# Scatters declared as writes to rows of their own, one wait ahead of the readers, and the routing's counts four slots later

## The chip, the core and the metric

The kernel runs on one core of a Trainium2 chip. The time is that of one execution on the device, in microseconds (us). The engines are PE (matrix multiply, with PEld for its weight loads), DVE (vector), ACT (scalar), POOL (GpSimd, which also issues the indirect DMAs) and SP (which issues the plain DMAs). Each engine takes its own instructions in the order in which they were written, and waits on semaphores for the others and for DMAs.

## The reference

Three stages follow one another, on 3072 tokens of width 384:

```python
# attention with a decaying state, over 4 batches, 8 heads, 768 steps, head width 48
for t in range(S):
    cur = einsum('bhd,bhe->bhde', u * k_t, v_t)
    y[t] = einsum('bhd,bhde->bhe', r_t, state + cur)
    state = w_t * state + einsum('bhd,bhe->bhde', k_t, v_t)
# mixture of 8 experts, each token to one of them
logits = x @ w_gate + modality_bias[modality_id]
e_idx, gate_w = argmax(logits), softmax(logits)[e_idx]
for e in range(8):
    mask = e_idx == e
    out[mask] = gate_w[mask] * (relu(x[mask] @ w1[e]) @ w2[e])
# three projections, their maximum, and a last matmul
h = maximum(maximum(x @ v1, x @ v2), x @ v3); h = maximum(h, ...)
return h @ v_out
```

## The kernel before

**Attention** works on 24 tiles of 128 tokens (`attention`, loop over `i`). In iteration `i` the DVE scans the decays of tile `i + 2` (L729), finishes the output `x` of tile `i - 1` (L814), and PE forms the scores of tile `i + 1` (L761) and the output of tile `i` (L789). POOL has four things per tile: it masks the scores `am` of tile `i + 1` (L765, twice), multiplies `nat` of tile `i + 2` (L692, L693), and scales `nat` of tile `i + 1` by its sums `sh` (L702). `output(i)` on PE needs the masked `am`; the next tile's `x` (L814) needs L702. So a POOL that is late holds up both PE and DVE.

**Routing** runs beside it in batches of tiles (`route_batch`, batches of 8, 8, 3, 2 and 3 tiles). A batch is a generator, and `slot()` calls in each iteration advance it by a few steps; a `SLOT` that it yields ends the slot. On DVE it finds each token's expert, on PE it counts the tokens of each expert ahead of this one (L264, L265, into `cum`), and from that DVE computes `places`: the row that each token has in a list ordered by expert. POOL then writes for each tile 128 pairs (token, weight) into those rows of the DRAM tensor `order` by one indirect DMA (`scatter`, L293). At most two tiles are scattered per iteration, one in the middle and one at the end (`do_scatters(1)`). `order` has been filled once with a value out of bounds by a plain DMA from `zt`.

**Readers of `order`.** In iteration 21 (`e - 3`), `first_ids(0)` issues what is left of the first 16 tiles' scatters and reads the first ids by indirect gathers into `oi_all` (L1094); `first_rows` then gathers the token rows `xin` (L1105). After the attention, `chain` scatters the last 8 tiles. Then `first_block` gathers the ids `oe` of the extra tile `X` (L1094, index `idxx` from L371), its rows `xin`, and transposes them on PE (`x_part`, L1113) between two halves of the second expert tile's matmuls.

**The experts' blocks.** `first_block` runs the 8 experts' two matmuls over 13 tiles of 256 tokens; `second_block` runs the three projections and the last matmul over 512 tokens at a time. Each 128 tokens of the result go to `ob` on ACT (L1205) and by an indirect DMA of POOL to their rows of `out` (L1206).

Every scatter to `order`, and every one to `out`, writes a tensor whose rows are only known when it runs, so by the tracking of accesses each waits until the one before has landed.

Of the kernel before, what the change touches and what calls it, by code (L numbers as in the profile page):

```python
# [33 lines left out]
W2_FIRST = range(8)  # L34
RATE = (2, 6, 4)
LEAD = 2
GAP = 1

V_MIX = [(1, 6), (0, 0), (0, 1), (1, 7), (0, 2), (0, 3), (1, 8), (0, 4), (0, 5), (1, 9)]
V_OPS = (0, 7, 6, 1, (2, 2, 1, 0), 7, 3)  # L40
# [6 lines left out]
def kernel(ctx: ExitStack, tc: tile.TileContext, rkw_t, v_t, vrk, u, modality, w_gate, bias, w1, w2, v1, v2,  # L47
                              v3, v_out, out):
    nc = tc.nc
    PE, DVE, ACT, POOL, SP = nc.tensor, nc.vector, nc.scalar, nc.gpsimd, nc.sync  # L50
    B, NC, _, D, _, HP, _ = rkw_t.shape
    H, S = 2 * HP, NC * 128
    NT, DM = out.shape
    E, _, F = w1.shape
    F2 = v1.shape[1]
    NTILE = NT // 128
# [11 lines left out]
    NG = -(-E * TW // 128)  # L68
# [22 lines left out]

    xs = dram.tile([NT, DM], F32, name="xs")
    x2t = dram.tile([NTILE // 2, 128, KD, TW], F32, name="x2t")
    order = dram.tile([E * NT, 2], I32, name="order")
    lgps = lgpool.tile([128, 512], F32, name="lgps")

# [19 lines left out]
    idg = ct([128, NTILE, 2], I32, "idg")  # L116
# [17 lines left out]
    places = ct([128, NTILE], I32, "places")  # L134
# [8 lines left out]
    def constants_rest(es):  # L143
        tmp = pool(es, "ctmp", 1)
        mi = tmp.tile([NTILE, 128, 2], I32, name="mi")

        def loads():
            SP.dma_start(out=b0, in_=bias.rearrange("m e -> (m e)")[None, :].to_broadcast([128, 2 * E])
                         .rearrange("p (m e) -> p m e", m=2))
            SP.dma_start(out=mi, in_=modality.bitcast(I32).rearrange("(t p a) -> t p a", t=NTILE, a=2))  # L150

        def rows():

            mf = tmp.tile([NTILE, 128], F32, name="mf")
            msk = tmp.tile([128, NTILE, E], I32, name="msk")
            DVE.tensor_copy(mf, mi[:, :, 0])
            zt = tmp.tile([128, 2 * E * NT // 128], I32, name="zt")
            POOL.memset(zt, OOB)
            SP.dma_start(out=order.rearrange("(p f) a -> p (f a)", p=128), in_=zt)
            yield  # L160
            ps = lgps[:, 288:288 + NTILE]
            PE.transpose(out=ps, in_=mf, identity=ident[0:NTILE, 0:NTILE])
            on = tmp.tile([128, 128], F32, name="on")
            POOL.memset(on, 1.0)
            yield
            DVE.tensor_copy(msk, ps.unsqueeze(2).to_broadcast([128, NTILE, E]))
            POOL.tensor_copy(ones_bf, on)
            yield
            DVE.tensor_copy(brow, b0[:, 0:1, :].to_broadcast([128, NTILE, E]))
            POOL.affine_select(out=sut_bf, in_=ones_bf, pattern=[[1, 128]], compare_op=ALU.is_gt, fill=0.0, base=0,  # L170
                               channel_multiplier=-1)
            yield
            DVE.copy_predicated(brow, msk, b0[:, 1:2, :].to_broadcast([128, NTILE, E]))
            iota(iota8, [[1, E]])
            iota(ebase, [[NT, E]])
            yield
            iota(iota24, [[TW, NTILE // 2]])
            iota(pidx, [[0, 1]], 0, 1)
            iota(pids, [[128, 2 * EARLY]], 0, 1)
            POOL.memset(zero8, 0.0)  # L180
            POOL.memset(idg, 0)
            yield
            POOL.iota(idg[:, :, 0], pattern=[[128, NTILE]], base=0, channel_multiplier=1)
            iota(iota256, [[1, TW]])
            yield
            iota(posm, [[128, NTILE]], 0, 1)
            iota(posl.rearrange("p (t a) -> p t a", a=2), [[TW, NTILE // 2], [0, 2]], TW - 1)
            yield
            POOL.memset(oi_all, OOB)
            POOL.memset(oe, OOB)  # L190
            for d in d0c.values():
                yield
                POOL.memset(d, 1.0)
                POOL.memset(d[:, :, 0:1], 0.0)
        return loads, rows


    carry = {"t": None}
# [38 lines left out]
    scatters = []  # L237

    def route_batch(batch, then=(), lead=0):

        t0, nb = batch
        for _ in range(lead):
            yield SLOT
        lg = cut("lg", nb, E)
        DVE.tensor_tensor(out=lg, in0=logits[:, t0:t0 + nb, :], in1=brow[:, t0:t0 + nb, :], op=ALU.add)
        yield
        oh = cut("oh", E, nb + 1, BF16, E * (NBMAX + 1))
        ohx = cut("ohx", E, nb + 1, BF16, E * (NBMAX + 1))
        if t0:
            DVE.tensor_copy(oh[:, :, 0], carry["t"])  # L250
        else:
            DVE.memset(oh[:, :, 0:1], 0.0)
        got = []
        yield from argmax_onehot(oh[:, :, 1:nb + 1].rearrange("p e c -> p c e"), lg, nb, "r", got)
        ex = cut("ex", nb, E)
        ACT.activation(out=ex, in_=got[0], func=ACTF.Exp)
        DVE.tensor_tensor_scan(out=ohx.rearrange("p e c -> p (e c)"), data0=d0c[nb].rearrange("p e c -> p (e c)"),
                               data1=oh.rearrange("p e c -> p (e c)"), initial=0.0, op0=ALU.mult, op1=ALU.add)
        carry["t"] = ohx[:, :, nb]
        for _ in range(lead and GAP):  # L260
            yield SLOT
        yield
        cum = lgps[:, 192:192 + E * nb].rearrange("p (e c) -> p e c", e=E)
        PE.matmul(cum, lhsT=sut_bf, rhs=oh[:, :, 1:nb + 1], start=True, stop=False)  # L264
        PE.matmul(cum, lhsT=ones_bf, rhs=ohx[:, :, 0:nb], start=False, stop=True)  # L265
        got = [gen() for gen in then]
        for gen in got:
            next(gen)
        for _ in range(lead and GAP):
            yield SLOT  # L270
        yield
        for gen in got:
            yield from gen
        sm = cut("sm", nb, 1)[:, :, 0]
        DVE.tensor_reduce(out=sm, in_=ex, axis=AX.X, op=ALU.add)
        yield
        DVE.tensor_scalar(out=sm, in0=sm, scalar1=1e-9, scalar2=None, op0=ALU.add)
        yield
        DVE.reciprocal(idg[:, t0:t0 + nb, 1].bitcast(F32), sm)
        yield  # L280
        pc = cut("pc", E, nb, F32, E * NBMAX)
        DVE.tensor_tensor(out=pc, in0=cum, in1=ebase.unsqueeze(2).to_broadcast([128, E, nb]), op=ALU.add)
        yield
        DVE.tensor_tensor(out=pc, in0=pc, in1=oh[:, :, 1:nb + 1], op=ALU.mult)
        yield
        pf = cut("pf", nb, 1)[:, :, 0]
        DVE.tensor_reduce(out=pf, in_=pc.rearrange("p e c -> p c e"), axis=AX.X, op=ALU.add)
        yield
        pi = places[:, t0:t0 + nb]
        DVE.tensor_copy(pi, pf)  # L290

        def scatter(c):
            POOL.indirect_dma_start(out=order[:, :], out_offset=bass.IndirectOffsetOnAxis(ap=pi[:, c:c + 1], axis=0),  # L293
                                    in_=idg[:, t0 + c, :], in_offset=None, bounds_check=E * NT - 1, oob_is_err=False)
        scatters.extend([lambda c=c: scatter(c) for c in range(nb)])

    def do_scatters(n=NTILE):
        for sc in scatters[:n]:
            sc()
        carry["scattered"] = carry.get("scattered", 0) + len(scatters[:n])  # L300
        del scatters[:n]
# [721 lines left out]
    class Experts:  # L1023
# [167 lines left out]
        def m2(self, ids):  # L1191
# [11 lines left out]
            def done(q):  # L1203
                ob = self.next_of("ob")
                ACT.activation(out=ob, in_=ps[q][:, 0:DM], func=ACTF.Copy, scale=ids[q][:, 1:2].bitcast(F32))  # L1205
                POOL.indirect_dma_start(out=out[:, :], out_offset=bass.IndirectOffsetOnAxis(ap=ids[q][:, 0:1], axis=0),  # L1206
                                        in_=ob, in_offset=None, bounds_check=NT - 1, oob_is_err=False)
            n = len(ids)

            early = range(1)  # L1210
# [50 lines left out]

    def first_ids(j):
        do_scatters(max(0, NG - carry["scattered"]))
        for q in (2 * j, 2 * j + 1):
            ex.gather_ids(oi_all[:, q, :], idxg[:, q:q + 1])

# [36 lines left out]
    def until(what):  # L1303
        for got in work:
            if got == what:
                return

    def first_block(vw):
# [6 lines left out]
        for s, cur in enumerate(seq):  # L1315
# [16 lines left out]
                    vw(V_OPS[2])  # L1332
            if s == EARLY - 1:
                until("X")
                for half in range(2):
                    ex.gather_ids(X["oi"][half], idxx[:, half:half + 1])
                rows_of(X)
                until("rows")
                ids_of(EARLY)
                rows_of(T[EARLY])  # L1340
                until("end")
                ids_of(EARLY + 1)
# [47 lines left out]
    def rest():  # L1390
# [3 lines left out]
        with tc.If(lastv > 0):  # L1394
            badv = nc.values_load(ctl[0:1, 62:63], min_val=0, max_val=1)
            with tc.If(badv > 0):
                with ExitStack() as es:
                    attention_general(es)
                with ExitStack() as es:
                    run(plan(es))  # L1400
            with ExitStack() as es:
# [109 lines left out]
```

## Time and profile before

| | |
|---|---|
| median of 3 runs | 824.42 us (823.46 to 825.88) |
| profiled execution | 823.74 us, span from first to last instruction 821.7 us |
| PE busy | 736.3 us, 90% of the span |
| DVE busy | 516.8 us, 63% |
| ACT busy | 313.8 us, 38% |
| POOL busy | 350.4 us, 43% |
| mean granted clock of PE | 0.93 of full speed |

The attention lies in the first 245 us or so, the first block reaches to about 550 us, the second block to 805 us. The shares are averages over these three: PE is nearly always busy in the two blocks, and in the attention DVE is.

### The profile page before, as it was taken

The numbers are of one execution on the slowest core, as the hardware profiler recorded it, in microseconds if no ns is written. First come the engines' busy times: TensorE is split into PE (matmuls) and PEld (weight loads), VectorE is DVE, ScalarE is ACT, GpSimd is POOL, SyncE is SP. The second block draws the span as 40 slices with busy tenths as digits, with TensorE's granted clock in tenths as the row PEclk, the third lists the DMA queues.
The fourth block names the chain that finished last, engine by engine and source line by source line (L and its number), as shares of the span: only waits on it lengthen the run. The fifth ranks groups of instructions, "written<-read, shape, count | busy, mean of one in ns | idle before, by whom it ended". The sixth has DMA issues, their size and how long they took to land. (4 is left out here: it accounts for less than half of the span.)

```text
span 821.7 us, 13030 instructions
## 1 busy us (share of the span) xinstructions
PE 736.3 (90%) x4737; PEld 663.8 (81%) x4746; DVE 516.8 (63%) x975; ACT 313.8 (38%) x705; POOL 350.4 (43%) x386
## 2 busy tenths in 40 slices
PE   6889897777859599999999999899999999999991
PEld 3778787667749598999999998788898988889891
DVE  5899996599748278777778887962414234142320
ACT  5556444234303145566566653331221222122110
POOL 7598665655572367565557543521020100102000
PEclk8699887879669899999999999999999999999997
DMA  8778687458311132211111723301020100101000
GB/s 233 185 217 253 181 192 195 109 162 228 90 58 23 45 113 61 79 59 59 60 59 58 244 77 116 115 11 68 1 77 1 59 20 0 39 1 39 0 12 32
DMA packets 32382, 74.57 MB, mean 91 GB/s; under 512 B 5973, under 2 KB 19061, under 8 KB 32308
## 3 DMA queue, kind: packets, MB, share of 16 engines
q1 hardware_dynamic: 27508, 64.15, 28.3%
q0 software_dynamic: 4800, 9.49, 3.6%
q8 instruction: 39, 0.64, 0.4%
q14 instruction: 35, 0.29, 0.1%
HBM read 87.96 MB, written 14.38 MB: 125 GB/s over the span
## 5 line engine op out<-in xcount | busy, mean ns | idle before, releaser
L1186 DVE TENSOR_TENSOR w2r<-mm,w2r 128x512 f32<-128x512 f32 x72 | 49.7, 691 | 140.9 <-PE mm L1126 140.8
L1124 PE MATMUL mm<-w1h,vh 128*128 128x512 f32 x324 | 126.1, 389 | 3.4 <-DVE w2r L1186 3.4
L1206 POOL DMA_INDIRECT out_dram<-w2r,oi_all x24 | 26.1, 1086 | 241.6 <-ACT w2r L1205 201.3
L1126 PE MATMUL mm<-w1h,vl 128*128 128x512 f32 x324 | 127.6, 394 | 0.0
L1125 PE MATMUL mm<-w1l,vh 128*128 128x512 f32 x324 | 127.0, 392 | 0.0
L1125 PE MATMUL mm<-hl,w2h 128*128 128x256 f32 x312 | 89.5, 287 | 3.2 <-DVE hl L1138 3.1
L1126 PE MATMUL mm<-xh,w1l 128*128 128x256 f32 x312 | 90.1, 289 | 1.4 <-DVE w1l L484 1.4
L1126 PE MATMUL mm<-hh,w2l 128*128 128x256 f32 x312 | 89.4, 286 | 0.9 <-DVE w2l L484 0.6
L1124 PE MATMUL mm<-hh,w2h 128*128 128x256 f32 x312 | 89.7, 288 | 0.0
L1124 PE MATMUL mm<-xh,w1h 128*128 128x256 f32 x312 | 88.5, 284 | 0.0
L1125 PE MATMUL mm<-xl,w1h 128*128 128x256 f32 x312 | 88.3, 283 | 0.2 <-issue 0.2
L789 PE MATMUL yb<-nat,am 128*128 128x56 f32 x384 | 57.8, 312 | 23.2 <-DVE lh L816 10.7
L789 PEld LDWEIGHTS yb<-nat,am 128*128 128x128 f32 x384 | 54.7, 226 | 25.8 <-POOL am L765 22.3
L1124 PEld LDWEIGHTS mm<-w1h,vh 128*128 128x128 f32 x324 | 60.8, 188 | 17.9 <-DVE w2r L1186 4.7
L484 DVE TENSOR_TENSOR w1l<-w1r,w1h 128x512 fp32r<-128x512 f32 x66 | 52.9, 855 | 35.2 <-ACT w1h L482 16.6
L1188 ACT CAST w2h<-w2r 128x512 fp32r<-128x512 f32 x36 | 22.3, 620 | 132.6 <-DVE w2r L1186 132.6
L1125 PEld LDWEIGHTS mm<-w1l,vh 128*128 128x128 f32 x324 | 60.8, 188 | 13.8
L1126 PEld LDWEIGHTS mm<-w1h,vl 128*128 128x128 f32 x324 | 60.9, 188 | 12.2
L484 POOL TENSOR_TENSOR w2l<-w2r,w2h 128x384 fp32r<-128x384 f32 x40 | 45.7, 1146 | 44.9 <-ACT w2h L482 43.9
L1125 PEld LDWEIGHTS mm<-hl,w2h 128*128 128x128 f32 x312 | 60.3, 193 | 4.8 <-DVE hl L1138 4.8
L1126 PEld LDWEIGHTS mm<-xh,w1l 128*128 128x128 f32 x312 | 59.7, 191 | 4.9 <-DVE w1l L484 4.9
L1126 PEld LDWEIGHTS mm<-hh,w2l 128*128 128x128 f32 x312 | 60.1, 193 | 1.9 <-DVE w2l L484 1.4
(242 smaller groups left out, 1758.3 us busy)
## 6 DMA issues: line engine op xcount, KB each, us to landing
w1r<-in_moe_w_dram SPq DMA_DIRECT2D x10, 1536.0 KB
w2r<-in_moe_w_dram SPq DMA_DIRECT2D x10, 1536.0 KB
nat<-in_vrk_dram SPq DMA_DIRECT2D x24, 608.0 KB
tq<-in_rkw_t_dram SPq DMA_DIRECT2D x46, 288.0 KB
stg<-in_moe_w_dram SPq DMA_DIRECT2D x18, 384.0 KB
vt<-in_v_t_dram SPq DMA_DIRECT2D x24, 192.0 KB
x2t<-raw SPq DMA_DIRECT2D x12, 384.0 KB
w1r<-x2t SPq DMA_DIRECT2D x12, 384.0 KB
```

The costliest lines, as they stand in the source:

```text
L484: eng.tensor_tensor(out=lo, in0=src, in1=hi.bitcast(F32), op=ALU.subtract)
L789: PE.matmul(yb[:, h * DV:(h + 1) * DV], lhsT=s["am"][:, 4 * (h % 2) + h // 2, :], rhs=s["v"][:, h, :], start=(h == 0), stop=(first and h = ...
L1124: PE.matmul(oc, lhsT=wh[:, kk, sl], rhs=xh[:, kk, :], start=first and kk == 0, stop=False)
L1125: PE.matmul(oc, lhsT=wh[:, kk, sl], rhs=xl[:, kk, :], start=False, stop=False)
L1126: PE.matmul(oc, lhsT=wl[:, kk, sl], rhs=xh[:, kk, :], start=False, stop=last and kk == nk - 1)
L1186: DVE.tensor_tensor(out=hv, in0=o, in1=hv, op=ALU.max)
L1188: ACT.copy(self.h2h[:, c, :], hv)
L1206: POOL.indirect_dma_start(out=out[:, :], out_offset=bass.IndirectOffsetOnAxis(ap=ids[q][:, 0:1], axis=0), in_=ob, in_offset=None, bounds_c ...
```

## The change

The scatters to `order` are put into a group whose members don't wait for each other, and so are the scatters to `out` where four are issued together (`apart`). Two instructions are new on POOL. `carry["filled"]` overwrites one column of `zt` ahead of the first scatter, so that it follows the fill's DMA, which reads `zt`. `settle` overwrites the `places` of the tiles scattered so far; each scatter reads its `places`, so this memset waits until all of them have landed, and the gathers of ids behind it on POOL come after. `GAP` becomes a pair: a batch's two matmuls that count (L264, L265) are written four slots behind the scan that they need, in place of one.

```diff
-GAP = 1
+GAP = (4, 1)
...
             SP.dma_start(out=order.rearrange("(p f) a -> p (f a)", p=128), in_=zt)
+            carry["filled"] = lambda: POOL.memset(zt[:, 0:1], 0)
...
-        for _ in range(lead and GAP):
+        for _ in range(lead and GAP[0]):
             yield SLOT
         yield
         cum = lgps[:, 192:192 + E * nb].rearrange("p (e c) -> p e c", e=E)
...
-            POOL.indirect_dma_start(out=order[:, :], out_offset=bass.IndirectOffsetOnAxis(ap=pi[:, c:c + 1], axis=0),
-                                    in_=idg[:, t0 + c, :], in_offset=None, bounds_check=E * NT - 1, oob_is_err=False)
+            apart("order", POOL.indirect_dma_start(
+                out=order[:, :], out_offset=bass.IndirectOffsetOnAxis(ap=pi[:, c:c + 1], axis=0),
+                in_=idg[:, t0 + c, :], in_offset=None, bounds_check=E * NT - 1, oob_is_err=False))
...
+    def apart(group, ins):
+        tc.declare_no_dep(ins.ins, group=group, reason="other rows")
+        tc.add_to_no_dep_group(group, ins.ins)
+    def settle(a, b):
+        POOL.memset(places[:, a:b], 0)
     def do_scatters(n=NTILE):
+        if scatters and "filled" in carry:
+            carry.pop("filled")()
         for sc in scatters[:n]:
             sc()
...
+                if n == 4:
+                    apart("out", ins)
...
     def first_ids(j):
         do_scatters(max(0, NG - carry["scattered"]))
+        if j == 0:
+            settle(0, NG)
...
                 until("X")
+                settle(NG, NTILE)
                 for half in range(2):
                     ex.gather_ids(X["oi"][half], idxx[:, half:half + 1])
```

The rows below are instructions of POOL in the order in which they stand, with the semaphores that each waits for. `DMASW0` to `DMASW7` are eight semaphores that POOL's own DMAs take in turn, and `Pool`, `DVE` and `Activation` are the engines' (the number behind them is the core's). First, two tiles of the attention around the first scatters, before:

```order
L293 DMA order_68<-idg_82,places_102 24576x2
L765 AFFINE_SELECT am_1309<-am_1309 128x512 [waits Activation_49] x2
L692 TENSOR_TENSOR nat_1239<-nat_1239,u_b_156 128x384 [waits DMAHW3_49]
L693 TENSOR_TENSOR nat_1239<-nat_1239 128x384 [waits Pool_49]
L293 DMA order_68<-idg_82,places_102 24576x2 [waits DMASW0_49]
L702 TENSOR_TENSOR nat_1142<-nat_1142,sh_1363 128x448 [waits DVE_49,Activation_49]
L293 DMA order_68<-idg_82,places_102 24576x2 [waits DMASW1_49]
L765 AFFINE_SELECT am_1398<-am_1398 128x512 [waits Activation_49] x2
```

The same place now:

```order
L781 AFFINE_SELECT am_1303<-am_1303 128x512 [waits Activation_49] x2
L708 TENSOR_TENSOR nat_1235<-nat_1235,u_b_156 128x384 [waits DMAHW3_49]
L709 TENSOR_TENSOR nat_1235<-nat_1235 128x384 [waits Pool_49]
L163 MEMSET zt_430 128x1
L297 DMA order_68<-idg_82,places_102 24576x2 [waits DVE_49]
L718 TENSOR_TENSOR nat_1142<-nat_1142,sh_1361 128x448 [waits DVE_49,Activation_49]
L297 DMA order_68<-idg_82,places_102 24576x2
L781 AFFINE_SELECT am_1396<-am_1396 128x512 [waits Activation_49] x2
```

The first scatter stands one slot (half a tile) later, the waits of one scatter for the last are gone, and the memset of `zt` is new.

Second, iteration 21 with `first_ids(0)`, before and now:

```order
L693 TENSOR_TENSOR nat_2148<-nat_2148 128x384 [waits Pool_49]
L293 DMA order_68<-idg_82,places_102 24576x2 [waits DMASW5_49]
L293 DMA order_68<-idg_82,places_102 24576x2 [waits DMASW6_49]
L1094 DMA oi_all_103<-order_68,idxg_95 128x2 [waits DMASW7_49]
L1094 DMA oi_all_103<-order_68,idxg_95 128x2
L702 TENSOR_TENSOR nat_2051<-nat_2051,sh_2297 128x448 [waits DVE_49,Activation_49]
```

```order
L709 TENSOR_TENSOR nat_2146<-nat_2146 128x384 [waits Pool_49]
L297 DMA order_68<-idg_82,places_102 24576x2 [waits DMASW5_49]
L297 DMA order_68<-idg_82,places_102 24576x2 [waits DMASW6_49]
L297 DMA order_68<-idg_82,places_102 24576x2 [waits DMASW7_49]
L309 MEMSET places_102 128x16 [waits DMASW4_49,DMASW5_49,DMASW3_49,DMASW6_49,DMASW2_49,DMASW7_49,DMASW1_49,DMASW0_49]
L1110 DMA oi_all_103<-order_68,idxg_95 128x2 x2
L718 TENSOR_TENSOR nat_2049<-nat_2049,sh_2299 128x448 [waits DVE_49,Activation_49]
```

Three scatters are left here instead of two. Each still names a semaphore, but with 16 scatters on eight semaphores in turn it is that of the scatter eight places ahead of it, not of the last one. The memset of `places` waits for all eight.

Third, the last 8 scatters and the gather of `oe` for the extra tile, before and now:

```order
L293 DMA order_68<-idg_82,places_102 24576x2 [waits DMASW3_49]
L293 DMA order_68<-idg_82,places_102 24576x2 [waits DMASW4_49,DVE_49]
L293 DMA order_68<-idg_82,places_102 24576x2 [waits DMASW6_49,DMASW5_49]
L293 DMA order_68<-idg_82,places_102 24576x2 [waits DMASW7_49,DMASW6_49]
L1094 DMA oe_104<-order_68,idxx_101 128x2 [waits DMASW7_49,DVE_49]
```

```order
L297 DMA order_68<-idg_82,places_102 24576x2
L297 DMA order_68<-idg_82,places_102 24576x2 [waits DVE_49]
L297 DMA order_68<-idg_82,places_102 24576x2 [waits DMASW6_49]
L297 DMA order_68<-idg_82,places_102 24576x2 [waits DMASW7_49]
L309 MEMSET places_102 128x8 [waits DMASW4_49,DMASW5_49,DMASW3_49,DMASW6_49,DMASW2_49,DMASW7_49,DMASW1_49,DMASW0_49]
L1110 DMA oe_104<-order_68,idxx_101 128x2 [waits DVE_49]
```

Here too the waits of one scatter for the one ahead are gone and one wait for all of them stands ahead of the gather.

## Rows read from the trace of the kernel before

**Rows 1.** Windows: busy us of each engine (instructions), granted clock, DMA share, GB/s.

```profile
core 0: us, PE busy (x) PEld busy (x) DVE busy (x) ACT busy (x) POOL busy (x), PEclk, DMA share, GB/s
47.65:88.86 41.21, 36.66 (x336) 33.10 (x336) 40.59 (x82) 24.25 (x72) 35.80 (x41) 1.00 0.85 235
88.86:107.63 18.77, 16.62 (x113) 15.57 (x112) 18.29 (x46) 8.10 (x25) 11.73 (x11) 0.70 0.73 194
113.43:165.69 52.26, 40.83 (x294) 37.36 (x294) 36.84 (x70) 21.34 (x63) 29.09 (x33) 0.83 0.70 166
165.69:204.67 38.98, 30.51 (x234) 27.00 (x235) 37.81 (x96) 15.48 (x47) 22.77 (x21) 0.85 0.71 185
204.67:245.17 40.50, 28.92 (x152) 23.81 (x153) 25.19 (x59) 7.88 (x20) 25.58 (x30) 0.65 0.26 76
278.50:288.77 10.27, 1.21 (x8) 1.20 (x7) 0.00 (x0) 0.85 (x2) 6.09 (x8) 0.61 0.06 16
287.57:292.00 4.43, 4.43 (x25) 4.43 (x26) 2.75 (x7) 1.43 (x4) 3.66 (x6) 0.61 0.02 1
```

**Rows 2.** The scatters' line: durations (ns), idle before them (us, times), landing.

```profile
L293 POOL DMA_INDIRECT order<-idg,places x24: 971/1008/1746, 109.7 to 276.7; - x24
...
  DMA order<-idg,places: 52.6, 16
...
DMA to landing us min/median/max: 3.6/8.6/9.0
```

**Rows 3.** Waits of DVE from 113.43 to 165.69: us, times, longest.

```profile
DVE x L814 <- POOL nat L702: 7.1, 3, 3.8
DVE sh L698 <- POOL nat L693: 5.6, 3, 2.1
```

**Rows 4.** Timeline of POOL, one tile of that stretch: start, us, instruction, idle before.

```profile
136.89 1.01 POOL L293 DMA_INDIRECT order<-idg,places  x1 [2.11 <-DMA order<-idg,places]
137.92 1.22 POOL L765 TENSOR_SCALAR_AFFINE_SELECT am<-am 128x512 f32<-128x512 f32 x2
139.11 0.99 POOL L692 TENSOR_TENSOR nat<-nat,u_b 128x384 f32<-128x384 f32 x1
...
145.53 1.01 POOL L293 DMA_INDIRECT order<-idg,places  x1 [4.36 <-DMA order<-idg,places]
146.57 0.94 POOL L702 TENSOR_TENSOR nat<-nat,sh 128x448 f32<-128x448 f32 x1
```

**Rows 5.** Timeline from the last scan (204.67) to the first block's first matmul.

```profile
207.40 1.07 ACT L764 COPY am<-mm 128x512 f32<-128x512 f32 x2 [0.23 <-PE mm L761]
...
222.28 1.01 POOL L293 DMA_INDIRECT order<-idg,places  x1 [0.43 <-DMA order<-idg,places]
...
226.48 0.97 POOL L293 DMA_INDIRECT order<-idg,places  x1 [3.20 <-DMA order<-idg,places]
230.41 1.04 POOL L1094 DMA_INDIRECT oi_all<-order,idxg  x1 [2.96 <-DMA order<-idg,places]
...
232.78 0.94 POOL L702 TENSOR_TENSOR nat<-nat,sh 128x448 f32<-128x448 f32 x1
...
235.79 1.19 POOL L1105 DMA_INDIRECT xin<-xs,oi_all  x1 [0.16 <-POOL xin L1101]
...
238.32 0.95 POOL L702 TENSOR_TENSOR nat<-nat,sh 128x448 f32<-128x448 f32 x1
...
240.25 0.56 DVE L814 TENSOR_TENSOR xe<-yb,nat 128x384 f32<-128x384 f32 x1 [0.95 <-PE yb L795]
...
245.17 0.38 PE L1124 MATMUL mm<-xh,w1h 128*128 128x256 f32 x1
```

**Rows 6.** Timeline around the extra tile.

```profile
257.78 0.16 DVE L371 SCALAR_TENSOR_TENSOR idxx<-pl_out,pl_gx 128x2 int32<-128x2 f32 x1
...
281.31 1.05 POOL L1094 DMA_INDIRECT oe<-order,idxx  x1 [3.63 <-DMA order<-idg,places]
...
287.57 1.54 PE L1113 MATMUL tp<-ident,xin 128*128 128x128 f32 x6 [9.06 <-DMA xin<-xs,oe]
```

**Rows 7.** Timeline at the end: the last result on ACT and its scatter on POOL.

```profile
804.54 0.58 ACT L1205 ACTIVATE w2r<-tp,oi_all 128x384 f32<-128x384 f32 x1 [2.54 <-PE tp L1201]
806.81 0.97 POOL L1206 DMA_INDIRECT out_dram<-w2r,oi_all  x1 [2.38 <-DMA out_dram<-w2r,oi_all]
```

More of the change, by code (lines that the diff above doesn't have):

```diff
@@ L268, in route_batch @@
             next(gen)
-        for _ in range(lead and GAP):
+        for _ in range(lead and GAP[1]):
             yield SLOT
@@ L1205, in done @@
                 ACT.activation(out=ob, in_=ps[q][:, 0:DM], func=ACTF.Copy, scale=ids[q][:, 1:2].bitcast(F32))
-                POOL.indirect_dma_start(out=out[:, :], out_offset=bass.IndirectOffsetOnAxis(ap=ids[q][:, 0:1], axis=0),
-                                        in_=ob, in_offset=None, bounds_check=NT - 1, oob_is_err=False)
+                ins = POOL.indirect_dma_start(out=out[:, :],
+                                              out_offset=bass.IndirectOffsetOnAxis(ap=ids[q][:, 0:1], axis=0),
+                                              in_=ob, in_offset=None, bounds_check=NT - 1, oob_is_err=False)
+                if n == 4:
+                    apart("out", ins)
             n = len(ids)
@@ L1398, in rest @@
                     attention_general(es)
+                settle(0, NTILE)
                 with ExitStack() as es:
```

## The prediction

> **What bounds the kernel now.** I read the windows by stage first, cut where a tile's first scan (L729) starts, then the scatters' line, then the waits of DVE and the timeline at the places where POOL stands still. In the attention before any scatter, six tiles take 41.21 us, 6.87 each, and DVE is busy for 40.59 of them: DVE is the bound there, with the DMA engines close behind at a share of 0.85 [rows 1]. When the first eight tiles are scattered, five tiles take 52.26 us, 10.5 each, and DVE is busy for only 36.84 [rows 1]. What happened is on POOL: in 16 places a scatter waited for the landing of the one before, 52.6 us in all, since a landing took 8.6 us at the median [rows 2]. In the tile shown the second scatter stands idle for 4.36 us and L702 comes only behind it [rows 4], and DVE's next tile needs L702: 7.1 us of DVE's idle time ended with L702 and 5.6 with L693, the other product of the same late POOL [rows 3]. So in this stretch the path runs over POOL's waits. It does so again from 204.67, where DVE is busy for 25.19 of 40.50 us [rows 1] and POOL waits 3.20 and 2.96 us between scatters and gathers before it comes to L702 [rows 5], and at the extra tile, where PE itself waits 9.06 us for rows whose ids were gathered behind the last scatter [rows 6]. In the two long blocks POOL's waits lie beside PE, but for the very last scatter [rows 7].
>
> **The change part by part.** Two scatters per tile remain as instructions of 1.01 us [rows 2]; what goes is the idle time ahead of them.
>
> *The scattered tiles, 113.43 to 165.69.* DVE was idle for 52.26 - 36.84 = 15.4 us, and 12.7 of these ended with POOL [rows 1, 3]. POOL's own work per tile, without waits, is 1.22 for the two L765, 0.99 for each of L692 and L693, 0.94 for L702 and 2.02 for two scatters, 6.2 us [rows 4], less than the 7.4 that DVE was busy per tile here. If DVE becomes the bound again, all 15.4 us go. Against that, the DMA engines were busy for 0.70 of 52.26, 36.6 us, and the same loads and scatters would have to fit in 36.8: two resources are nearly full at once. I take 7.85 us per tile, a gain of 13; the ends are 15.4 and the 5.3 of the first rival.
>
> *The counts four slots later.* PE no longer meets L264 ahead of the scan that it needs. But DVE is busy for 18.29 of 18.77 and 37.81 of 38.98 us around the first two batches [rows 1], so at most 1.65 us of idle time can go; I take 1. `places` and the number of the first expert come half a tile later, and one more scatter is left for iteration 21. If nothing covered the half tile it would cost 3.4 us once; the weights' loads stand an iteration behind, which covers it. Ends: a gain of 4, if what DVE does in small steps then meets POOL less often, and a loss of 3.4. The memset of `zt` and the two of `places` cost some 0.3 us each on POOL beside their waits, an estimate: the 0.16 us that an instruction starts behind its releaser [rows 5], and as much again for a column or a few of integers.
>
> *The end of the attention, from the last scan at 204.67.* The masked scores can start when ACT is done at 208.47, 3.8 us behind the scan [rows 5]. With POOL no longer a tile late, L765, L692 and L693 take it to 7.1. Three scatters, 1.3 us apart as issued, put the start of the last at 9.8. The new wait needs its landing: two scatters here stood 4.2 us apart, 222.28 and 226.48, with each waiting for the one before [rows 5], which gives 14.0, and 14.3 behind the memset. The two gathers take 2.4 as before (230.41 to 232.78), so L702 starts at 16.7. From it to the next L702 it took 5.5 (238.32), from there to `xe` 1.9, and from `xe` to the first matmul of the block 4.9 [rows 5]: 29.0 us in place of 40.5, a gain of 11.5. Ends: 13.5, if landing takes the 3.6 of the quickest and PE is at the higher clock level sooner, and 7, if it takes 8.6 [rows 2].
>
> *The extra tile.* Its ids need the last 8 scatters landed and `idxx`, which DVE has 12.6 us into the block (257.78) [rows 6]. The scatters, no longer 4 us apart, are then all but issued; with 1.3 for the last, 4.2 for landing and the 6.3 us from the gather of `oe` to PE's first transpose (281.31 to 287.57) the rows are there some 24 to 25 us into the block, and PE asks for them at 278.50, 33.3 into it. The whole wait of 9.06 goes. After it the granted clock averaged 0.61 over 4.43 us [rows 1], that is, partly at the lower level, which cost 4.43 x 0.39 = 1.7. Gain 10.8. Even a landing of 9.0 us leaves this slack; were there none, up to 9.06 would come back.
>
> *The scatters of the result.* Twenty-four of them lose waits, but PE doesn't wait for them. Only the last is on the path: ACT is done with it at 805.12 and it starts at 806.81 [rows 7]. It would start some 0.3 behind ACT; gain 1.4.
>
> The sum is 13 + 1 + 11.5 + 10.8 + 1.4 = 37.7 us. The profiled execution took 823.74 us, so 786.0; the median of the runs is 0.7 above it, so I say 786.5.
>
> **The rivals.** *POOL without waits gets in DVE's way.* DVE was busy for 6.77 us per tile without scatters and 7.37 with two [rows 1], so something of a scatter may already be paid on DVE. If each scatter stopped DVE for its whole 1.01 us, ten of them would turn 36.84 into 46.9 and leave 5.3 of the 15.4 us: 794. That it was 0.6 per tile and not 2.0 speaks against it; that POOL was idle for nearly half of this stretch (busy 29.09 of 52.26), so that the two met less often, speaks for it. The Trainium skill, "SBUF — State Buffer", section "Who interferes with whom", has a rule that would do this: GpSimd and VectorE share a pair of SBUF ports under an exclusive lock, and the second to come is blocked for the whole instruction. By that rule the rise of 0.6 us is what one would look for, though the trace does not show what caused it. Chance 0.16.
>
> *The new wait takes the place of the old.* The first memset of `places` waits for landings; at the median's 8.6 us in place of 4.2 the end of the attention gains 7 instead of 11.5: 791. For it: 8.6 is the median [rows 2]. Against it: the DMA share from 204.67 on is 0.26, against 0.70 where landings were slow [rows 1]. Chance 0.10.
>
> *Slower.* Scatters that nothing paces take the DMA engines from the attention's loads, and every tile waits for its data. To undo 37.7 us and add the 2.5 that a measurement of this kernel can tell (0.3%), each of 24 would have to cost the loads 40 / 24 = 1.7 us of all 16 engines. The share of 0.70 with two scatters per tile, below the 0.85 without [rows 1], speaks against a cost of that size. Then 827 or more. Chance 0.03.
>
> *No change.* The waits that were named were not what landed last, and others (loads, PE) end at the same times. The 12.7 us that DVE waited for POOL and the 9.06 of PE speak against it. Chance 0.02. *More than the sum:* DVE's small steps get shorter in the routing stretches too, and the ends above come together at 45 us: 779 or less. Chance 0.09.
>
> **How the numbers follow.** What I forecast, 780 to 793, has 0.60, and that is its own range; its price is the sum. With the two rivals above it and most of the one below, 777 to 802 leaves out less than 2 in 10; 802 is 5.3 for the scattered tiles, a loss of 2 for the counts, 7 for the end of the attention, 10.8 and 1.4. Faster by over 0.3%: 0.60 + 0.16 + 0.10 + 0.09 = 0.95; within it 0.02; slower 0.03.
>
> **What would show it.** After the change, the idle time of L297 (the scatters' new line) that ends with a DMA should be near zero; the five scattered tiles should take 39 us and DVE be busy for 95% of them; from the last scan to the first matmul of the block should be about 29 us, with one wait of some 3 us at the memset of `places`; the wait of PE at the extra tile should be gone and the clock stay at its higher level there; the last scatter should start within 0.3 us of ACT. I am wrong if DVE's busy time in the scattered tiles grows by as much as its idle time falls, if PE or DVE wait for loads there, or if the memset of `places` waits for 8 us.

## The result, and the profile after

The changed kernel took 790.72 us at the median (789.26 to 794.78, 4 runs), the kernel before, beside it, 825.15. The ratio is 0.9585, 95% interval 0.9535 to 0.9635. Run again beside some of its variants (e7, below), it was 0.9648 (0.9623 to 0.9673), and that is the figure for comparisons with them. The profiled execution took 794.78 us, the longest of the four, with a span of 792.5 in place of 821.7.

First the stages, cut where a tile's first scan (now L745) starts: six tiles before any scatter, three with the first routing ([rows 1] has two of them), the five scattered ones, four more, and from the last scan to the first block's first matmul.

```profile
45.83:87.05 41.22, 36.76 (x338) 33.10 (x336) 40.60 (x83) 24.14 (x72) 35.81 (x41) 1.00 0.85 232
87.05:111.97 24.92, 21.04 (x168) 19.30 (x167) 24.37 (x58) 10.99 (x34) 16.04 (x16) 0.86 0.66 181
111.97:152.57 40.60, 37.02 (x290) 34.13 (x289) 38.60 (x71) 21.01 (x62) 36.55 (x35) 0.83 0.90 198
152.57:191.56 38.99, 29.59 (x227) 26.87 (x226) 37.84 (x93) 16.00 (x48) 27.91 (x25) 0.84 0.79 201
191.56:225.37 33.81, 24.82 (x161) 20.21 (x160) 19.98 (x62) 7.85 (x20) 21.85 (x26) 0.73 0.38 85
```

The five tiles went from 52.26 to 40.60 us, and DVE is busy for 95% of them. But its busy time rose too, from 36.84 to 38.60, and POOL's to 36.55, 7.3 per tile. The end of the attention went from 40.50 to 33.81, less than I had said.

The scatters' line shows that the waits between scatters are gone, all 52.6 us of [rows 2]. What is left, 10.3 us in 2 places, is waited for by the two memsets of `places` (L309):

```profile
L297 POOL DMA_INDIRECT order<-idg,places x24: 972/1010/1864, 113.1 to 236.8; - x24
...
  issue: 4.4, 20
  DVE pl_cgs L374: 1.8, 1
...
  POOL places L309: 10.3, 2
...
DMA to landing us min/median/max: 3.3/5.6/11.5
```

Most of these 10.3 us fall where it hurts, as the timeline of the attention's end shows (compare [rows 5]):

```profile
194.67 0.96 SPq L1278 DMA_DIRECT2D w2r<-in_moe_w_dram  x2
...
202.23 0.98 POOL L297 DMA_INDIRECT order<-idg,places  x1 [0.30 <-issue]
...
202.71 0.37 SPq L1278 DMA_DIRECT2D w2r<-in_moe_w_dram  x1
...
210.02 0.11 POOL L309 MEMSET places<- 128x16 int32 x1 [6.82 <-DMA order<-idg,places]
210.80 1.05 POOL L1110 DMA_INDIRECT oi_all<-order,idxg  x1 [0.67 <-issue]
...
213.19 0.94 POOL L718 TENSOR_TENSOR nat<-nat,sh 128x448 f32<-128x448 f32 x1
...
214.17 0.56 DVE L830 TENSOR_TENSOR x<-yb,nat 128x384 f32<-128x384 f32 x1 [8.37 <-POOL nat L718]
...
225.37 0.38 PE L1140 MATMUL mm<-xh,w1h 128*128 128x256 f32 x1
```

The last of the first 16 scatters starts at 202.23 and the memset only at 210.02: 7.8 us. Behind it on POOL stand the gathers of ids and L718, and DVE waits 8.37 us for L718. The chain of work that ended last runs this way: the landing, the gathers, L718, DVE, PE. Three loads of w2 were issued close by.

At the extra tile, and at the last result ([rows 6, 7]):

```profile
241.51 0.10 POOL L309 MEMSET places<- 128x8 int32 x1 [3.51 <-DMA order<-idg,places]
...
258.57 0.82 PE L1129 MATMUL tp<-ident,xin 128*128 128x128 f32 x6
...
776.47 0.58 ACT L1221 ACTIVATE w2r<-tp,oi_all 128x384 f32<-128x384 f32 x1 [2.60 <-PE tp L1217]
777.33 0.97 POOL L1222 DMA_INDIRECT out_dram<-w2r,oi_all  x1 [2.21 <-ACT w2r L1221]
```

PE takes the extra tile's rows without a wait, where it had waited 9.06 us, and over the 4.43 us from there the granted clock was 1.00 (0.61 before). The last scatter starts 0.28 us behind the end of ACT (776.47 + 0.58), where it was 1.69.

The ledger of the spans, the change's first profile and a second one (e7, below) against the one of before; each stretch is a difference of two starts in the timelines. "The other routed tiles" are the three ahead of the five scattered ones and the four behind them:

| stretch | predicted gain | first | second |
|---|---|---|---|
| start to the scan of tile 11 | 0 | 1.8 | 0.0 |
| the five scattered tiles | 13 | 11.7 | 10.7 |
| the other routed tiles (counts) | 1 | -0.4 | -0.4 |
| last scan to the first matmul of the block | 11.5 | 6.7 | 6.9 |
| from there to the last result on ACT | 10.8 | 8.3 | 9.7 |
| the last result to the end | 1.4 | 1.1 | 1.3 |
| sum | 37.7 | 29.2 | 28.2 |

So 8.5 and 9.5 us of the sum are missing: nearly 5 at the end of the attention, 1.3 and 2.3 in the five tiles, 1.4 in the counts, and the rest in the blocks. By the medians the gain was 34.4 us in the first comparison, where the profiled execution was the slowest of the four, and 28.0 in the second.

### The profile page after: what moved, and what is told of

It reads as the page before. It is cut to its first block, busy times and chain, and to the rows that moved or that the text cites. A ratio compares the mean times of both kernels' runs of the same rounds, so it can differ in the third digit from the quotient of the medians.

```text
span 792.5 us, 13036 instructions
## 1 busy us (share of the span) xinstructions
PE 724.9 (91%) x4745; PEld 654.8 (83%) x4746; DVE 516.7 (65%) x975; ACT 313.5 (40%) x705; POOL 359.4 (45%) x389
## 4 chain that ended last, share of the span: by engine, by line
issue 37%; PE 23%; DVE 22%; DMA 7%; POOL 7%; ACT 2%; SPq 1%; POOLq 0%; ACTq 0%; DVEq 0%
PE mm L1142 7%; PE mm L1141 6%; PE mm L1140 6%; DMA tq<-in_rkw_t_dram 5%; POOL out_dram L1222 3%; DVE w1l L500 3%; DVE prod L745 2%; DVE prod L761 2%; DMA nat<-in_vrk_dram 1%; DVE rt L754 1%; DVE hl L1154 1%; DVE x L830 1%; DVE w2l L500 1%; DMA order<-idg,places 1%; DVE ya L528 1%
## 5 line engine op out<-in xcount | busy, mean ns | idle before, releaser
L1142 PE MATMUL mm<-w1h,vl 128*128 128x512 f32 x324 | 126.0, 389 | 0.0
L500 DVE TENSOR_TENSOR w1l<-w1r,w1h 128x512 fp32r<-128x512 f32 x66 | 52.1, 843 | 34.7 <-ACT w1h L498 34.6
L805 PE MATMUL yb<-nat,am 128*128 128x56 f32 x384 | 53.4, 299 | 16.4 <-DVE lh L832 13.9
L805 PEld LDWEIGHTS yb<-nat,am 128*128 128x128 f32 x384 | 51.0, 214 | 18.4 <-POOL am L781 9.0
L500 POOL TENSOR_TENSOR w2l<-w2r,w2h 128x384 fp32r<-128x384 f32 x40 | 45.7, 1146 | 45.0 <-ACT w2h L498 43.9
```

Of the source, the lines that this page charges most:

```text
L500: eng.tensor_tensor(out=lo, in0=src, in1=hi.bitcast(F32), op=ALU.subtract)
L805: PE.matmul(yb[:, h * DV:(h + 1) * DV], lhsT=s["am"][:, 4 * (h % 2) + h // 2, :], rhs=s["v"][:, h, :], start=(h == 0), stop=(first and h = ...
L1142: PE.matmul(oc, lhsT=wl[:, kk, sl], rhs=xh[:, kk, :], start=False, stop=last and kk == nk - 1)
```

## The experiments

All are variants of the changed kernel unless said otherwise; ratios are to the kernel before, run on the same chip. There were three chips: one for e1, e2, e3 and e6, one for e4, e5, e7 and e8, and one for e9. So e7 stands beside e4, e5 and e8 directly, and beside the others only by the ratios. The medians of before were 823.5 to 824.4 us, so 0.001 is 0.8 us.

**The change once more (e7).**

> The change itself, for the comparison with its variants on one chip, and for one question: in its profiled execution the last block's matmuls of 128x384 came every 176.4 ns, against 173.6 before, and the stretch from the block's first matmul to the last result was 2 to 3 us longer than in the variants with the same code there. Theory: that belongs to the one execution, and here the pitch is 173.6 or less and the span about 790 us. Rival: it belongs to the change, and shows again. Ratio in both cases 0.9585 within 0.004.

Ratio 0.9648 (0.9623 to 0.9673), above the bound that I gave (0.9625); the span was 793.6, not 790. The last matmuls came every 172.9 ns (the mean over 14 of them in the timeline). From the first result on ACT to the last it was 254.0 us here, 253.9 before, and 255.4 in the first profile of the change. Of all eleven profiles only that one and e4's have 255.4, the others 253.9 to 254.6, with the same matmuls there. So these 1.5 us belong to the execution.

**The last 8 scatters tied again (e1).**

```diff
-            apart("order", POOL.indirect_dma_start(
+            ins = POOL.indirect_dma_start(
...
+            if t0 < NG:
+                apart("order", ins)
```

> The changed kernel with the last 8 scatters of order back in order, each waiting for the landing of the one before, as in the kernel before; the first 16 and the scatters of the result stay free. Theory (my sum): the extra tile was worth 10.8 us, so this kernel takes about 790.7 + 10.8 = 801.5 us, a ratio of 0.971 to the kernel before, and PE waits some 9 us for the extra tile's rows again. Rival: the two traces show only 8.3 us less from the first matmul of the block to the last result, so the wait was worth less than I said: 799 us, 0.968. Second rival: the extra tile's rows would now come in time anyway, since the block's first ids come earlier; then there is no wait at the extra tile and the time stays at 791 us, 0.958.

Ratio 0.9761 (0.9734 to 0.9788), with the change at 0.9648 in such a comparison. PE waits again, now 10.80 us:

```profile
251.09 0.97 POOL L297 DMA_INDIRECT order<-idg,places  x1 [4.55 <-DMA order<-idg,places]
255.54 0.97 POOL L297 DMA_INDIRECT order<-idg,places  x1 [3.48 <-DMA order<-idg,places]
...
266.35 1.54 PE L1131 MATMUL tp<-ident,xin 128*128 128x128 f32 x6 [10.80 <-DMA xin<-xs,oe]
```

From the block's first matmul to the last result it takes 561.5 us, against 549.7 in e7 and 551.1 in the first profile: 10.4 to 11.8, as the sum had it (10.8). Both rivals are out. By the ratios the whole differs by 0.0113, or 9.3 us; in the profiles the end of the attention was 3 us shorter in e1 (30.55) than in e7 (33.57).

**No scatter in the five tiles (e6), and the same kernel timed (e8).** The two scatters of an iteration, one in the middle and one at its end, become two at each of these places, from iteration 17 on (the same edit at both):

```diff
-                if i < NTILE - 3:
-                    do_scatters(1)
+                if 17 <= i < NTILE - 3:
+                    do_scatters(2)
```

> The changed kernel with no scatter in the five tiles that had two each; they are issued two to a slot from iteration 17 on. Theory: the scatters on POOL lengthen DVE's instructions beside them (the scan L745 took 1.60 us there and 1.48 in the tiles without scatters; DVE was busy 7.7 us per tile), so without them the five tiles take 36 to 38 us instead of 40.6 and L745 falls back to 1.48 or less. Rival: what lengthens DVE there is POOL's other work (L709, L781), which keeps its place: L745 stays at 1.6 us and the five tiles at 40 us or more. Where the scatters come in pairs, later, the tiles get longer by what two cost; the whole is within 1% of the change.

The five tiles took 35.41 us in place of 40.60, 7.08 each, for 8 scatters less. The rows of DVE and POOL in these tiles, by line and shape (busy us, mean ns), of the change:

```profile
L745 DVE TENSOR_TENSOR_SCAN prod<-tq,d1f 128x512 f32<-128x512 f32 x6 | 9.6, 1596 | 0.0
L761 DVE TENSOR_TENSOR_SCAN prod<-tq,d1r 128x511 f32<-128x511 f32 x5 | 8.5, 1702 | 0.0
L730 DVE TENSOR_SCALAR tq<-tq 128x512 f32<-128x512 f32 x5 | 3.7, 743 | 0.0
...
L781 POOL TENSOR_SCALAR_AFFINE_SELECT am<-am 128x512 f32<-128x512 f32 x10 | 7.0, 718 | 2.2 <-ACT am L780 2.2
L718 POOL TENSOR_TENSOR nat<-nat,sh 128x448 f32<-128x448 f32 x5 | 4.7, 943 | 0.1
```

and of e6, with its windows:

```profile
112.93:148.34 35.41, 31.88 (x290) 28.74 (x292) 34.90 (x71) 21.40 (x63) 31.18 (x27) 1.00 0.89 237
148.34:188.87 40.53, 30.64 (x238) 27.29 (x240) 39.40 (x93) 15.37 (x47) 35.11 (x34) 0.86 0.78 183
...
L745 DVE TENSOR_TENSOR_SCAN prod<-tq,d1f 128x512 f32<-128x512 f32 x6 | 8.8, 1460 | 0.0
L761 DVE TENSOR_TENSOR_SCAN prod<-tq,d1r 128x511 f32<-128x511 f32 x5 | 6.3, 1259 | 0.0
L730 DVE TENSOR_SCALAR tq<-tq 128x512 f32<-128x512 f32 x5 | 2.8, 555 | 0.0
...
L781 POOL TENSOR_SCALAR_AFFINE_SELECT am<-am 128x512 f32<-128x512 f32 x10 | 10.7, 1090 | 3.7 <-ACT am L780 3.7
L718 POOL TENSOR_TENSOR nat<-nat,sh 128x448 f32<-128x448 f32 x5 | 7.4, 1486 | 0.0
```

DVE is 3.7 us less busy (38.60 to 34.90) and 1.5 less idle; 5.19 in all, 0.65 per scatter. Without scatters it is POOL that is long: L718 takes 1.49 us and L781 1.09, and L761 on DVE 1.26. With them L718 takes 0.94, L781 0.72 and L761 1.70. It isn't the same two that meet: in e6 L781 falls beside L761 in all five tiles, and L718 beside the first scan L745 in three (rows in the last section); in the change L718 falls beside L761 in three. So the scatters moved POOL against DVE, and DVE, which has no time to spare, was the one that paid. The theory holds in its size, and the rival (POOL's other work) is right in a way: L761 is long beside L718, but only where a scatter has shifted POOL. In the four tiles after, where e6 issues 13 scatters and the change 4, it took 40.53 us against 38.99. The whole, 781.38 us in its one run, was further below the change than the 1% that I allowed.

> The kernel with no scatter in the five tiles and two to a slot from iteration 17 on, timed. Theory, from its one profile (781.4 us): scatters cost DVE time where DVE is the bound, and cost little where the split of the weights and PE set the pace; and the first 16 are all issued before the settle, which waits 1.3 us there. So it is 9 us faster than the change, a ratio of 0.948 to the kernel before. Rival: that one execution was a good one, and the true gain over the change is below 4 us, 0.954 or more.

Ratio 0.9543 (0.9520 to 0.9566), 0.0105 or 8.6 us less than the change: the theory's difference, and more than twice what the rival allows; the ratio itself is higher than I gave (0.948), as is that of the change beside it. The rival's first half holds: e6's 781.38 lies below all five runs here (783.88 to 789.32). Here the settle waits hardly at all, since the last of the 16 scatters starts 5.2 us behind the last scan (189.90) and not 10.7:

```profile
195.13 0.98 POOL L297 DMA_INDIRECT order<-idg,places  x1 [0.30 <-issue]
200.23 0.11 POOL L309 MEMSET places<- 128x16 int32 x1 [0.84 <-DMA order<-idg,places]
```

and the last scan to the block's first matmul takes 25.80 us. The chain that ended last no longer goes through the settle, but through a load of w2 and DVE, which splits the weights (L500):

```profile
193.59 5.75 DMA w2r<-in_moe_w_dram
199.87 1.80 DVE w1l L500 x3
```

Some of the gain is given back: from the block's first matmul to the last result it is 553.1 us here, against 549.7 in e7; why isn't shown. This and e9 below, which can't be told from it, are the fastest versions that I have.

**The counts four slots behind the scan in place of one.** That is three slots later, and an iteration has six. The move was made alone on the kernel before (e2), and taken back in the change (e3) and in the late pairs (e9). The edit in e3 and e9 is this line; e2 puts `(4, 1)` for the 1 of the kernel before:

```diff
-GAP = (4, 1)
+GAP = (1, 1)
```

> The kernel before with the counts four slots later and nothing else; every scatter still waits for the landing of the one before. Theory (my sum): a gain of 1 us, ratio 0.999, within what can be measured. Rival: the counts come late into the end of the attention and cost up to 3.4 us, ratio 1.004, with the last scan to the first matmul of the block longer than 40.5 us. Second rival: PE and DVE meet less often in the routed tiles, a gain of 4 us, ratio 0.995.

Ratio 1.0020 (1.0004 to 1.0037): 1.7 us slower, hardly more than the noise; the first rival in kind. The end of the attention grew from 40.50 to 43.77 us, 3.3, the loss of the lower end that I gave for places that come half a tile late; the four tiles before it gained 1.2.

> The changed kernel with the counts where they were, one slot behind instead of four. Theory (my sum): 1 us slower than the change, 791.7 us, ratio 0.959 to the kernel before. Rival: the places come half a tile earlier, the last scatters of the first 16 start before the settle's slot, and the wait at the memset of places (6.82 us in the change) shrinks by about 3 us: 788 us, 0.955. Second rival: PE waits for the scan at the counts in every routed tile, the five scattered tiles take over 42 us instead of 40.6, and the time is 793 us or more, 0.961.

Ratio 0.9643 (0.9621 to 0.9666), the same as the change in e7. In parts it was not the same: the five tiles took 44.23 us and the four after them 44.13, against 41.59 and 39.03 in e7; the end of the attention took 28.80 against 33.57, with 4.25 us of wait at the memset. Both rivals are right in the stretches that they name, and they cancel, with 1.8 us less in the blocks. But the second is not right in its reason: in the five tiles there is no counting matmul at all (they stand at 98.0 and 169.3 us), and DVE is both busier than in e7 (40.96 us against 39.61) and more idle. In the four tiles after, PE does wait 2.9 us for the counts.

Together with e2, each half of the change stands alone (us; the last column has the change's first profile and e7):

| | before | counts alone (e2) | scatters alone (e3) | both |
|---|---|---|---|---|
| five scattered tiles | 52.26 | 52.89 | 44.23 | 40.60, 41.59 |
| the four after them | 38.98 | 37.75 | 44.13 | 38.99, 39.03 |
| last scan to the block's first matmul | 40.50 | 43.77 | 28.80 | 33.81, 33.57 |
| from there to the last result | 559.4 | 560.2 | 547.9 | 551.1, 549.7 |
| ratio | 1 | 1.0020 | 0.9643 | 0.9585, 0.9648 |

So the gain is that of the scatters; the counts only move time from stretch to stretch.

> The kernel with the scatters in late pairs, and the counts back where they were, one slot behind instead of four. With two scatters in each of the five tiles this move lengthened the tiles 14 to 19 by about 3 us and 19 to 23 by 5, and shortened the end of the attention by 5, so that the time stayed the same (ratios 0.9643 and 0.9648). Theory: its loss in the tiles is that the scatters then meet DVE's long instructions (L761 took 2.1 us there), its gain at the end that the settle waits less. Without scatters in the five tiles these take 36 us as before, the settle waits hardly at all either way, and the time is that of the late pairs within 2 us, 0.952 to 0.957. Rival: the loss is PE's, which waits for the scan at the counts in every routed tile; then the tiles 14 to 23 take 5 us or more longer here too, with nothing to gain at the end: 0.960 or more.

Ratio 0.9544 (0.9520 to 0.9568), the same as e8, with 35.47 us for the five tiles. So the loss of e3 in the five tiles came with the scatters there and not with the counts. The four tiles after took 42.95 against 41.00, and PE waited 9.0 us for the counts in them (3.19 and 5.78): the rival's wait is there, but the tiles 14 to 23 are 1.5 us longer than in e8, not 5.

**The loads of w2 out of the settle's way (e4).**

```diff
-                   (NG + 5, "mid"): [bind(first_load, 1, 1)],
-                   (NG + 5, "end"): [bind(first_load, 1, 2), bind(ex.open_rows, wes)],
+                   (NG + 5, "end"): [bind(ex.open_rows, wes)],
...
-                   (e - 2, "mid"): [bind(first_load, 1, 3)],
+                   (e - 1, "uterm"): [bind(first_load, 1, 1), bind(first_load, 1, 2), bind(first_load, 1, 3)],
```

> The changed kernel with three of the four loads of w2 (384 KB each, issued at 194.67, 194.67 and 202.71 us in the change) moved into the last iteration, behind the settle; no scatter is moved. Theory: these loads hold the DMA engines while the last three scatters of the first 16 are on their way, so that the memset of places waits 6.82 us, landing 7.8 us behind the start of the last one; without them the landing takes some 4.2 us, the wait 3 us, and the time is about 3 us less than the change, a ratio of 0.955 to the kernel before. Rival: the queue of the scatters itself takes 7 to 8 us for the three; the wait stays at 6 to 7 us and the time at that of the change, or above it, since the loads then stand beside the gathers of the block's rows: 0.9585 to 0.962.

```profile
201.46 0.97 POOL L297 DMA_INDIRECT order<-idg,places  x1 [0.30 <-issue]
207.04 0.11 POOL L309 MEMSET places<- 128x16 int32 x1 [4.62 <-DMA order<-idg,places]
```

From the last scatter's start to the memset it is 5.6 us in place of 7.2 (e7), 7.8 (the change) and 8.4 (e5). But e1, whose code up to here is that of the change and whose loads stand at the same places (194.78 and 202.66 us), had 6.1, and e8 had 5.1 with two of the loads issued 2.1 us ahead of its last scatter. So one profile without the loads doesn't show that they are part of it. 4.2 wasn't reached with them or without. The end of the attention is 1.6 us shorter than in e7 (31.98), and the ratio, 0.9642 (0.9621 to 0.9662), doesn't tell it from the change.

**The settle behind L718 (e5).**

```diff
-        do_scatters(max(0, NG - carry["scattered"]))
...
-                   (e - 3, "uterm"): [bind(first_ids, 0)],
+                   (e - 3, "uterm"): [lambda: do_scatters(max(0, NG - carry["scattered"]))],
...
+                   (NG + 5, "end"): [bind(first_load, 1, 2), bind(ex.open_rows, wes), bind(first_ids, 0)],
```

> The changed kernel with the first settle and the two gathers of ids moved on POOL behind L718 of the same iteration; the three scatters ahead of it stay. Theory: the wait at the memset is paid because L718 stands behind it (DVE waited 8.37 us for L718 there); with L718 ahead, part of the wait lies beside the last output of the attention, and the last scan to the first matmul of the block takes 30 to 32 us instead of 33.8: a gain of 2 to 3 us, ratio 0.955. Rival: the block's rows, not L718, are what ends last there, and these depend on the settle, which comes no earlier; then the time stays at that of the change, 0.9585, or grows by the 1 us of L718.

Ratio 0.9672 (0.9659 to 0.9686), and the end of the attention took 33.58 us: the rival's number. Its reason isn't shown, since something else took L718's place: L718 no longer waits, but the masks (L781) do, which now stand behind the settle, and PE with them:

```profile
211.89 0.11 POOL L309 MEMSET places<- 128x16 int32 x1 [6.42 <-DMA order<-idg,places]
...
215.77 3.82 PE L805 MATMUL yb<-nat,am 128*128 128x56 f32 x16 [7.84 <-POOL am L781]
```

From this memset to the block's first matmul it was 14.6 us here, 15.3 in the change, 15.7 in e7, and 14.5 to 15.9 in e1, e3 and e4, while the memset itself lay 14.3 to 19.0 us behind the last scan. So in these kernels the settle, with what stands behind it on POOL, sets the block's start; whether the last output or the block's rows end last, this run can't tell. In e6, e8 and e9 the distance is about the same (15.3 to 16.5), but there the settle hardly waits, and in e6 and e8 the chain that ended last goes past it.

## Why the prediction was right, and where its sum was too large

The direction, and the places of the gains, were those forecast. The time lies 4 us above the number that I gave in the first comparison (790.7) and 9 in the second (795.5, e7). The first is within the 780 to 793 that I forecast, the second only within the wider 777 to 802, where the rivals' times are. In the profiles the sum of 37.7 us was 8.5 and 9.5 too large. (The 786.0 and 0.7 of its last step make 786.7; I wrote 786.5.) By its terms:

- **The scattered tiles** (13 said, 11.7 and 10.7 found). The waits between scatters went, and DVE became the bound, as said. "If DVE becomes the bound again" stands on the 7.37 us per tile that DVE was busy before; it came to 7.72, and without scatters it is 6.98 (e6). That is the mechanism of the first rival: a scatter costs 0.65 us of these tiles, not the 1.01 of its price, and part of it was paid before the change already. The rival's price was too high in its count as well: it took ten scatters, two per tile, and the stretch has eight now and had seven before. POOL's own work was priced too low, at 6.2 us per tile; it came to 7.3, since a scatter's issue took 1.39 us at the mean there and not 1.01, and L709 1.58 and not 0.99. That DVE pays could have been read before: in the trace of the kernel before, DVE's second scan took 1253 ns at the mean in the six tiles without scatters and 1656 in the five with them ([rows 1] has these stretches, not the line). The Trainium skill, "SBUF — State Buffer", section "Who interferes with whom", says that a VectorE instruction with two SBUF inputs contends with a GpSimd instruction that reads SBUF. The trace agrees in kind: beside each other in the change, L718 keeps its 0.94 and L761 takes 2.35 (rows in the last section).
- **The counts** (1 said). Alone they cost 1.7 us (e2), within the ends that I gave (a loss of 3.4, a gain of 4); with the scatters free they change nothing that can be measured (e3, e9). In e3 that is because what they give to the tiles they mostly take from the end of the attention.
- **The end of the attention** (11.5 said, 6.7 and 6.9 found). This is the term that failed most: the step "the new wait needs its landing: two scatters here stood 4.2 us apart". That spacing is from scatters that went out one at a time. The last three of the change, issued 1.3 us apart, landed 3.4, 5.3 and 7.7 us behind their starts; so 4.2 was enough for the first of them only. The memset came 7.8 us behind the last scatter, nearer to the second rival's 8.6 than to 4.2, and the gain was nearly the 7 of that rival. No run showed less than 5.1 at this memset (at the second one it was 4.7 in the change). Of the 4.8 us missing, 0.9 are the last scatter's start (10.7 us behind the scan in place of 9.8), 3.3 the landing with the memset (7.8 in place of 4.5), and 0.6 the way from the memset to the first matmul (15.3 in place of 14.7). Whether the loads of w2 are part of it is not shown (e4 against e1). What a landing there waits for stays open.
- **The extra tile** (10.8 said). e1 shows 10.4 to 11.8 for it alone, and both parts of the term are in the trace, the wait and the clock. The ledger's 8.3 has the 1.5 us of that execution's last part in it.
- **The last scatter** (1.4 said): 1.1 and 1.3 to the end; up to its start it gained the 1.4 (0.28 us behind ACT, where it was 1.69).
- **Slower, or no change**: neither is left. The DMA share rose from 0.70 to 0.90 in the five tiles, and DVE was idle for only 2.0 us of them.

So two of the rivals came true in part beside the forecast, and a sum of best steps had no room for both. The rows gave a landing of 4.2 at that place and 8.6 at the median [rows 2]; with three scatters to be on their way at once, where the rows had one, the term should have stood between the two.

## What to carry to other kernels

A wait that is taken away between writes and put once in front of their readers is worth what the waits cost on the path, less the last landing: issue the last writes early enough, and little of it is left (6.82 us of wait in the change, 0.84 in e8). An engine that no longer waits also moves against its neighbours: look at the mean time of the same instruction in stretches with and without the freed work, on both engines, before taking a busy time as a floor. Where freed instructions are put matters as much as that they are free: the first 8 scatters cost 5.2 us in their five tiles, and the next four tiles took 9 more for 1.5 (e6). DVE is busy for 97% of those four with and without them, so its busy share doesn't say where they are cheap, and why they are isn't shown; it took a run to find out.

## What the runs showed of the hardware

Which engine pays where DVE and POOL meet differs from place to place. Two tiles of the change, DVE's second scan (L761) and its clamp (L730) beside POOL:

```profile
130.55 1.01 POOL L297 DMA_INDIRECT order<-idg,places  x1 [0.16 <-DVE rt L754]
131.28 2.35 DVE L761 TENSOR_TENSOR_SCAN prod<-tq,d1r 128x511 f32<-128x511 f32 x1
131.59 0.94 POOL L718 TENSOR_TENSOR nat<-nat,sh 128x448 f32<-128x448 f32 x1
132.70 1.74 POOL L297 DMA_INDIRECT order<-idg,places  x1 [0.17 <-issue]
133.77 0.91 DVE L730 TENSOR_SCALAR tq<-tq 128x512 f32<-128x512 f32 x1
...
139.92 0.94 POOL L718 TENSOR_TENSOR nat<-nat,sh 128x448 f32<-128x448 f32 x1
141.03 1.01 POOL L297 DMA_INDIRECT order<-idg,places  x1 [0.17 <-issue]
141.21 1.22 DVE L761 TENSOR_TENSOR_SCAN prod<-tq,d1r 128x511 f32<-128x511 f32 x1
142.57 0.43 DVE L730 TENSOR_SCALAR tq<-tq 128x512 f32<-128x512 f32 x1
```

Where L718 falls into the scan, the scan takes 2.35 us, about 1.22 and the whole of L718 more. The scatter that starts within this scan takes 1.74 and ends 0.81 us behind the scan's end, and the clamp beside it takes 0.91 and not 0.43. That isn't so each time: at 183.46 a scatter within a scan took 1.75, and the clamp beside it 0.43. The scatter that starts 0.18 us ahead of the scan costs neither anything.

Without scatters, in e6, it is mostly POOL that pays:

```profile
122.50 1.22 DVE L761 TENSOR_TENSOR_SCAN prod<-tq,d1r 128x511 f32<-128x511 f32 x1
122.71 2.20 POOL L781 TENSOR_SCALAR_AFFINE_SELECT am<-am 128x512 f32<-128x512 f32 x2 [0.21 <-ACT am L780]
...
126.46 1.59 DVE L745 TENSOR_TENSOR_SCAN prod<-tq,d1f 128x512 f32<-128x512 f32 x1
126.92 1.85 POOL L718 TENSOR_TENSOR nat<-nat,sh 128x448 f32<-128x448 f32 x1
```

Here too DVE's scan starts first, as at 131.28 above, and yet it is L781 (two in 1.22 us without a meeting) and L718 (0.94) that get most of the length. What differs is that above, a scatter is still running on POOL when the scan starts. Over all eleven profiles there are 14 places where that is so and L718 starts some 0.3 us into the second scan: L718 took 0.94 or 0.95 us in each, and the scan 2.34 to 2.36 (4.46 once). In the three places where L718 starts 0.15 to 0.40 into that scan and no scatter is running, L718 took 1.85 and the scan 1.28 to 1.52. With a scatter running and L718 starting later, 0.51 and 0.54 us into the scan (e2, e7), both paid: 1.87, and 1.67 and 1.70. So a scatter just ahead goes with DVE's paying; how it brings that about is not shown.

In the five tiles the granted clock averaged 1.00 in e6 (7.1 us per tile) and 0.83, that is partly at the lower level, in the change (8.1) and in the kernel before (10.5, [rows 1]). About the same matmuls (x290) kept PE busy for 31.88 us in e6 and 37.02 in the change.
